# A three-number VectorE instruction in a new shape, and the first batch's softmax weights four slots later, in a fused attention and MLP kernel

## The chip, the cores and the metric

The kernel runs on one core of a Trainium2 chip. The metric is the time of one execution on the device in microseconds (us), as the median of several executions. Ratios are the mean time of one kernel's runs over that of the kernel before in the same rounds on the same chip, so they are not quite the ratio of the medians quoted beside them.

The engines are called PE (TensorE matmul), PEld (its weight load), DVE (VectorE), ACT (ScalarE) and POOL (GpSimd).

## The reference

```python
scores = scale * q @ k.T                          # 8 batches, 8 heads, 576 x 576, depth 64
thresh = max(scores, axis=-1) - tau
scores = where(scores >= thresh, scores, -1e9)
attn = exp(scores - max(scores)); attn /= sum(attn) + 1e-9
x = (attn @ v), heads side by side                # 4608 x 512
h = x @ w_in;  out = (h - tanh(h)) @ w_out        # hidden width 2048
```

## The kernel before

The work is a list of 288 score tiles (128 query rows by 576 keys), nine for each pair of heads. One slot of the schedule handles several tiles at different stages: in slot s the scores of tile s+8 are made, the threshold shift `nb` of tile s+7, the kinked scores `z` of tile s+5, and the transposes and the exponential of tile s; the product with V follows two slots later. In the first batch these last three are done four slots earlier. From the second batch on, the MLP of the batch before is mixed in, so PE has much more to do. GpSimd splits K and Q into two fp16 halves, swaps halves of K^T (`kS`), casts V, and casts the MLP's weights.

The parts that the change touches:

```python
mx = const.tile([P, 3], F32, name=f"mx{i}")       # row maxima: tile A in column 0, tile B in column 1
...
def shift(i):                                     # once for two tiles A and B, or for one tile M
    kd = kind(i % TPP)
    if kd == "A":
        return
    n = 3 if kd == "B" else 1
    mx = mxs.pop(i)
    nb = st_pool.tile([P, 3], F32, name="nb", tag="nb")
    nc.vector.tensor_scalar(
        out=nb[:, 0:n], in0=mx[:, 0:n], scalar1=-1.0, scalar2=tau,
        op0=ALU.mult, op1=ALU.add,
    )
    nbs[i] = nb[:, n // 2 : n // 2 + 1]
    if kd == "B":
        nbs[i - 1] = nb[:, 0:1]
...
for i in range(NTILE + 3):
    at = i - 4 if i < HPAIR * TPP else i          # slot of the weights; the first batch is 36 tiles
    atts.setdefault(at + LAG, []).append(i)
    if i < NTILE:
        wts.setdefault(at, []).append(i)
...
```

## Time and profile before

| | before |
|---|---|
| median of the first three runs | 549.77 us (549.69 to 550.95) |
| the run that was profiled | 543.29 us, span of the core 541.5 us |
| PE, DVE, ACT, POOL busy | 94, 82, 81, 54% |
| `nb` instructions | 160, 45.6 us in all, 136 to 1240 ns each |

### The profile page before, as it was taken

How to read it: one execution, taken by the hardware profiler on the slowest of the kernel's cores; microseconds unless marked ns; L12 is line 12 of the kernel's file. 1: busy time of each engine (PE TensorE's matmuls, PEld its weight loads, DVE VectorE, ACT ScalarE, POOL GpSimd, SP SyncE). 2: the span in 40 equal slices, each digit the busy share in tenths (PEclk: the TensorE clock that was granted, in tenths of full speed). 3: DMA queues.
4: the chain of work that ended last, by engine and by line, in shares of the span. 5: the costliest groups of instructions: out<-in, count | busy, mean ns of one | idle time of the engine just before them, and what ended most of it. 6: DMA issues, size and time to landing. Idle time of an engine off the chain costs nothing.

```text
span 541.5 us, 12959 instructions
## 1 busy us (share of the span) xinstructions
PE 506.7 (94%) x4704; PEld 288.0 (53%) x4771; DVE 445.9 (82%) x1203; ACT 438.3 (81%) x628; POOL 291.1 (54%) x390
## 2 busy tenths in 40 slices
PE   5999898989999999999999999999999999999997
PEld 3666565555555555555555555555555455444444
DVE  4999988989988999889888998899888887554440
ACT  4999888999898989899888989898989989533330
POOL 7999996767555666666545654566665620000000
PEclk9999999999999999999999999999999999999999
DMA  7554657999898998889999899698969975301113
GB/s 207 174 183 146 205 179 141 184 186 170 196 186 151 185 188 189 161 179 184 185 185 183 182 187 197 154 181 185 188 165 182 197 148 105 101 20 40 39 41 78
DMA packets 204768, 85.76 MB, mean 158 GB/s; under 512 B 172320, under 2 KB 197152, under 8 KB 204704
## 3 DMA queue, kind: packets, MB, share of 16 engines
q1 hardware_dynamic: 204112, 84.51, 72.6%
q8 instruction: 37, 0.61, 0.5%
q10 hardware_dynamic: 592, 0.43, 0.3%
q14 instruction: 27, 0.22, 0.1%
HBM read 36.70 MB, written 9.44 MB: 85 GB/s over the span
## 4 chain that ended last, share of the span: by engine, by line
PE 62%; DVE 24%; issue 5%; ACT 5%; DMA 3%; SPq 0%; DVEq 0%; ACTq 0%; POOL 0%
PE psY L510 18%; PE psH L484 16%; PE psS L319 13%; DVE sc L329 12%; PE psO L429 4%; DVE g L503 4%; PE psS L309 3%; PE ps_k L233 2%; PE psHt L484 2%; ACT pT L392 2%; ACT z L363 2%; DVE yo L520 2%; DMA qT<-qhl 2%; DVE nb L343 2%; DVE kT L256 1%
## 5 line engine op out<-in xcount | busy, mean ns | idle before, releaser
L329 DVE TENSOR_SCALAR_CACHE_REDUCE sc<-psS 128x576 f32<-128x576 f32 x288 | 215.7, 751 | 17.7 <-PE psS L319 10.4
L363 ACT ACTIVATE z<-sc,nb 128x576 bf16<-128x576 f32 x256 | 194.0, 771 | 22.9 <-DVE nb L343 22.4
L262 POOL COPY kS<-kT 64x1152 f16<-64x1152 f16 x62 | 70.9, 1143 | 132.6 <-DVE nb L343 130.9
L510 PE MATMUL psY<-w_out_sb,g 128*128 128x512 bf16 (+1 forms) x551 | 137.4, 373 | 4.1 <-DVE yo L520 1.6
L400 ACT ACTIVATE pT<-zT 128x1152 f16<-128x1152 bf16 (+1 forms) x130 | 139.1, 1070 | 0.0
L484 PE MATMUL psH<-xT,w_in_sb 128*128 128x512 bf16 x455 | 119.2, 379 | 7.2 <-DVE g L503 3.9
L319 PE MATMUL psS<-kT,qT 128*128 128x512 f16 (+1 forms) x512 | 104.9, 286 | 8.5 <-DVE sc L329 6.5
L497 ACT ACTIVATE th<-psH 128x512 f32<-128x512 f32 x128 | 75.5, 590 | 38.3 <-PE psH L484 37.7
L319 PEld LDWEIGHTS <-qT 128*128 128x128 f16 x1024 | 72.8, 97 | 58.1 <-issue 11.6
L503 DVE SCALAR_TENSOR_TENSOR g<-th,psH 128x512 bf16<-128x512 f32 x128 | 87.3, 682 | 19.0 <-ACT th L497 18.8
L319 PE MATMUL psS<-kS,qT 128*128 128x512 f16 x496 | 101.4, 286 | 0.0
L510 PEld LDWEIGHTS <-g 128*128 128x128 bf16 x592 | 50.7, 98 | 58.2 <-issue 5.7
L484 PEld LDWEIGHTS <-w_in_sb 128*128 128x128 bf16 x576 | 49.2, 98 | 59.7 <-issue 6.0
L429 PEld LDWEIGHTS <-pT 128*128 128x128 f16 x1280 | 55.7, 98 | 25.3 <-issue 1.7
L429 PE MATMUL psO<-vb,pT 128*128 128x65 bf16 x1280 | 61.2, 193 | 0.3
L343 DVE TENSOR_SCALAR nb<-mx 128x3 f32<-128x3 f32 (+1 forms) x160 | 45.6, 285 | 2.3
L186 POOL TENSOR_TENSOR khl<-kraw,khl 128x576 f16<-128x576 f32 x31 | 39.7, 1281 | 2.6
L186 POOL TENSOR_TENSOR qhl<-qraw,qhl 128x576 f16<-128x576 f32 x31 | 39.7, 1280 | 2.6
L392 ACT ACTIVATE pT<-psZ 128x640 f16<-128x640 bf16 (+1 forms) x54 | 35.4, 658 | 5.2 <-PE psZ L383 4.8
L256 DVE COPY kT<-ps_k 128x1152 f16<-128x1152 f16 x31 | 23.4, 756 | 13.3 <-PE ps_k L233 13.3
L520 DVE COPY yo<-psY 128x512 f32<-128x512 f32 (+1 forms) x33 | 22.5, 681 | 12.2 <-PE psY L510 7.6
L444 DVE TENSOR_TENSOR osb<-psO,rc 128x256 bf16<-128x256 f32 x64 | 27.2, 425 | 2.2
(78 smaller groups left out, 504.6 us busy)
## 6 DMA issues: line engine op xcount, KB each, us to landing
vraw<-in_v_dram SPq DMA_DIRECT2D x32, 256.0 KB, 3.5
out_dram<-yo SPq DMA_DIRECT2D x32, 256.0 KB, 2.8
kraw<-in_k_dram SPq DMA_DIRECT2D x31, 256.0 KB, 3.1
qraw<-in_q_dram SPq DMA_DIRECT2D x31, 256.0 KB, 3.9
wt<-in_moe_w_in_dram SPq DMA_DIRECT2D x8, 512.0 KB, 4.8
wt<-in_moe_w_out_dram SPq DMA_DIRECT2D x8, 512.0 KB, 3.9
zT<-z SPq DMA_TRANSPOSE x104, 3.5
kraw<-in_k_dram SPq DMA_DIRECT2D x32, 32.0 KB, 3.1
```

What stands on the lines that cost most here:

```text
L186: nc.gpsimd.tensor_tensor(out=hl[:, :, 1, :], in0=x, in1=hl[:, :, 0, :], op=ALU.subtract)
L262: nc.gpsimd.tensor_copy(out=o, in_=i)
L319: nc.tensor.matmul(out=ps[:, dst], lhsT=lhs, rhs=kk[:, src], start=(n == 0), stop=(n == 1),)
L329: nc.vector.tensor_scalar(out=sc, in0=ps[:, lo : lo + S], scalar1=SC, scalar2=None, op0=ALU.mult, op1=ALU.max, accum_out=mx[:, c : c + 1],)
L343: nc.vector.tensor_scalar(out=nb[:, 0:n], in0=mx[:, 0:n], scalar1=-1.0, scalar2=tau, op0=ALU.mult, op1=ALU.add,)
L363: nc.scalar.activation(out=z, in_=sc, func=ACT.Prelu, bias=nb, scale=1.0, alpha=STEEP)
L400: nc.scalar.activation(out=pt[:, 0 : n * P], in_=zts.pop(i)[:, 0:n, :], func=ACT.Exp)
L429: nc.tensor.matmul(out=po[:, (j - 1 - 5 * hh) + ab, :], lhsT=pt[:, blk * P : (blk + 1) * P], rhs=vb[:, hh, c, :], start=(n == 0), stop=(n ...
L484: nc.tensor.matmul(out=ps, lhsT=w_in_sb[:, c, n * P : (n + 1) * P], rhs=xs[m][:, c, :] if m < B else xR[:, c, :, :], start=(c == 0), stop= ...
L497: nc.scalar.activation(out=th, in_=ps, func=ACT.Tanh)
L503: nc.vector.scalar_tensor_tensor(out=gs[m][:, n, :], in0=th, scalar=-1.0, in1=ps, op0=ALU.mult, op1=ALU.add,)
L510: nc.tensor.matmul(out=ps, lhsT=gs[m][:, n, ms * P : (ms + 1) * P], rhs=w_out_sb[:, n, cols], start=(n == 0), stop=(n == DF_C - 1),)
```

## The change

It has two parts. The first writes the shift of a pair of tiles as rows: three numbers in each of two input rows, two in each of three output rows, of which only the first two outputs are used. The maxima get eight columns so that the input rows exist. The second moves the weights of the first batch to the slots that the other batches use.

```diff
-        mx = const.tile([P, 3], F32, name=f"mx{i}")
+        mx = const.tile([P, 8], F32, name=f"mx{i}")
...
-        n = 3 if kd == "B" else 1
         mx = mxs.pop(i)
-        nb = st_pool.tile([P, 3], F32, name="nb", tag="nb")
+        nb = st_pool.tile([P, 9], F32, name="nb", tag="nb")
+        o, m = nb[:, 0:1], mx[:, 0:1]
+        if kd == "B":
+            o = nb.rearrange("p (a b) -> p a b", b=3)[:, :, 0:2]
+            m = mx.rearrange("p (a b) -> p a b", b=4)[:, :, 0:3]
         nc.vector.tensor_scalar(
-            out=nb[:, 0:n], in0=mx[:, 0:n], scalar1=-1.0, scalar2=tau,
-            op0=ALU.mult, op1=ALU.add,
-        )
-        nbs[i] = nb[:, n // 2 : n // 2 + 1]
+            out=o, in0=m, scalar1=-1.0, scalar2=tau, op0=ALU.mult, op1=ALU.add
+        )
         if kd == "B":
-            nbs[i - 1] = nb[:, 0:1]
+            nbs[i - 1], nbs[i] = nb[:, 0:1], nb[:, 1:2]
+        else:
+            nbs[i] = nb[:, 0:1]
...
-        at = i - 4 if i < HPAIR * TPP else i
+        at = i - 0 if i < HPAIR * TPP else i
```

## The prediction

> **What bounds the kernel now.** I read the page first, then the list of groups, the rows of one line, the timeline around single instructions, the chain, and the waits by stretch. The page says that no engine has much room:
>
> ```profile
> PE 506.7 (94%) x4704; PEld 288.0 (53%) x4771; DVE 445.9 (82%) x1203; ACT 438.3 (81%) x628; POOL 291.1 (54%) x390
> ...
> L343 DVE TENSOR_SCALAR nb<-mx 128x3 f32<-128x3 f32 (+1 forms) x160 | 45.6, 285 | 2.3
> ```
>
> The reader is to see two things. PE is nearly always busy, so whatever DVE saves can only be taken out of PE's few holes. And an instruction that makes three numbers per partition takes 285 ns on average, far too much for its size. Busy time by stretch:
>
> ```profile
> core 0: us, PE busy (x) PEld busy (x) DVE busy (x) ACT busy (x) POOL busy (x), PEclk, DMA share, GB/s
> ...
> 16.00:60.00 44.00, 40.11 (x565) 28.45 (x564) 42.47 (x122) 42.58 (x69) 41.69 (x52) 1.00 0.57 178
> 60.00:125.00 65.00, 57.87 (x634) 36.24 (x641) 58.11 (x164) 58.71 (x89) 49.98 (x63) 1.00 0.76 166
> 125.00:460.00 335.00, 323.68 (x3020) 180.79 (x3070) 302.65 (x831) 300.05 (x413) 186.87 (x238) 1.00 0.89 177
> 460.00:542.00 82.00, 75.36 (x406) 36.25 (x409) 33.99 (x57) 28.48 (x46) 0.00 (x0) 0.99 0.18 53
> ```
>
> There are three regimes. From 16 to 60 us (the first batch, attention alone) ACT and DVE are both near 97% and PE has 3.9 us of holes. From 125 to 460 PE has 11.3 us of holes in 335. After 460 there are no `nb` instructions and PE runs alone.
>
> Now the rows of line 343, where the duration spreads over a factor of nine, and one instance in the timeline:
>
> ```profile
> L343 DVE TENSOR_SCALAR nb<-mx x160: 136/169/1240, 10.4 to 459.4; 128x3 f32<-128x3 f32 x128, 128x1 f32<-128x1 f32 x32
> ```
>
> ```profile
> 270.78 1.28 POOL L186 TENSOR_TENSOR qhl<-qraw,qhl 128x576 f16<-128x576 f32 x1
> ...
> 271.01 1.07 DVE L343 TENSOR_SCALAR nb<-mx 128x3 f32<-128x3 f32 x1
> ...
> 271.99 0.74 DVE L329 TENSOR_SCALAR_CACHE_REDUCE sc<-psS 128x576 f32<-128x576 f32 x1
> ...
> 272.67 0.68 DVE L520 COPY yo<-psY 128x512 f32<-128x512 f32 x1
> ...
> 273.27 0.67 DVE L503 SCALAR_TENSOR_TENSOR g<-th,psH 128x512 bf16<-128x512 f32 x1
> ...
> 273.99 0.38 PE L484 MATMUL psH<-xT,w_in_sb 128*128 128x512 bf16 x1 [0.70 <-DVE g L503]
> ```
>
> The GpSimd subtraction ends at 272.06 and the `nb` that began inside it ends at 272.08. Then three DVE instructions stand back to back and PE idles 0.70 us for the last of them. I went through all 160 in the timeline. The 32 of one element take 0.14 to 0.15 us, every one. Of the 128 of three elements, 82 take 0.15 to 0.20 us and 46 take 0.25 us or more; nearly all of those 46 end within 0.04 us after a GpSimd instruction ends. With 0.165 us for an undisturbed one, the three-element rows (128 x 0.320 = 41.0 us) hold 41.0 - 128 x 0.165 = 19.8 us of waiting for GpSimd: some 5 us of it before 70 us, the rest later.
>
> [...] the 3-to-3 form is held up, 46 times in 128, until a GpSimd instruction ends; the 1-to-1 form never is, 0 times in 32.
>
> **Part one, the new shape.** The instruction order shows the same 160 `nb`, now 128x3x2 out, with an input of two rows of three. [...] It computes six numbers in place of three (two are used), which I put at the 0.14 us of the one-element form or slightly more: 0.15 us. DVE work removed: 128 x (0.320 - 0.15) = 21.8 us, so L343 should fall from 45.6 to about 24 us and DVE from 446 to about 424.
>
> What does this buy? Not 21.8 us: I take only what lies on the chain that ended last. Its pieces on line 343 longer than an undisturbed one are:
>
> ```profile
> 23.39 0.60 DVE nb L343
> ...
> 34.68 0.68 DVE nb L343
> ...
> 108.79 0.67 DVE nb L343
> ...
> 153.38 0.43 DVE nb L343
> ...
> 209.28 1.24 DVE nb L343
> ...
> 271.01 0.44 DVE nb L343
> ```
>
> and after these 206.99 (0.32), 329.84 (0.44) and 389.07 (0.43). Where the piece is a cut of a longer instruction (153, 271, 330, 389) the whole piece is waiting; from the others I take 0.165 off. Sum after 70 us: 0.50 + 0.43 + 0.16 + 1.08 + 0.44 + 0.44 + 0.43 = **3.5 us**. Before 70 us: 0.44 + 0.52 = **0.96 us**. The other waits lie where DVE afterwards waits for PE anyway. Since the chain without these pieces is still a chain of the program, 4.4 us is about the most that this part can give while the order and the other durations stay.
>
> **Part two, the first batch's weights four slots later.** The transposes of tile i (line 383), the exponential (392) and the product with V (429) move from slot i-4 to slot i for the first 36 tiles. No instruction is added; only the order on PE and ACT changes. Now the transposes come one slot after the ACT instruction that makes `z`, and PE[...] stands waiting. Waits from 16 to 60 us:
>
> ```profile
> PEld L383 <- ACT z L363: 5.0, 14, 0.7
> ...
> PE psS L319 <- DVE sc L329: 2.1, 6, 0.5
> PE psZ L383 <- ACT z L363: 1.4, 4, 0.4
> ```
>
> After the change `z` is five slots old and these waits should be gone. The bound is then ACT: on the chain an ACT `z` takes 0.67 us to the next instruction and a `pT` 0.50 to 0.60. From 16 to 60 us it runs 35 `z` and 34 `pT`: 35 x 0.67 + 34 x 0.54 = 41.8 of 44 us. So only 2.2 us are to be had there. A little more lies in slots -4 to -1, which the timeline puts at 13.1 to 18.5 us: 5.4 us with `pT` in them, by my estimate 4.6 us if they hold only scores; slots 32 to 35, now with `z` alone, get their `pT` back and stay at about 5.2 us. I take **2.5 us** for the first batch with both parts together, the 0.96 us included. Sum: 3.5 + 2.5 = 6.0 us, and 0.4 us for shorter undisturbed `nb` on the chain: 549.8 - 6.4 = **543.4 us**.
>
> **Rivals.**
> First, DVE relief is worth far more, as DVE is at 97% in the first batch and 90% later: if most of PE's holes from 16 to 460 us (3.9 + 7.1 + 11.3 = 22.3 us) close, the time falls to 530 or lower. For it: DVE frees 22 us. Against it: most of those holes name other causes (`psS` waiting for `sc` where no `nb` was held, `psH` for `xT`, `pT`).
> Second, ACT takes over at once and nothing comes of it: about 549. For it: ACT already has 97% in the first batch and 90% later. Against it: the chain has PE at 62%, DVE at 24% and ACT at 5%.
> Third, the deferral costs: ACT runs short of work in slots -4 to -1 and has the same `pT` to do later, so the first batch grows by 1 to 2 us and the sum is near 547.
> Fourth, a transfer: DMA share is 0.89 in the long stretch and `qT` by DMA lies on the chain twice, 5.55 and 3.98 us. But PE's waits for it are only a few tenths of a us, so I expect at most 1 us either way.
>
> **Range and chances.** The parts bound the gain at about 3.9 us (first batch) plus 4 (later) plus 1.5 (DMA and small things), so 540; if the deferral costs and the chain gives half, 547.5. Two per cent faster is below 538.8, past what I can add up: 10%. Slower by over 2% has no mechanism: 2%. Within: 88%.
>
> **What would show it.** L343 with a maximum below 0.25 us, a mean near 0.15, and a sum near 24; no `nb` that ends with a GpSimd instruction. DVE near 424 us. The waits of L383 for `z` before 60 us gone. The scores of tile 45 (`sc` at 64.75 us now) some 2.5 us earlier; the end of the last `nb` (459.4 now) some 6 us earlier; the stretch after it unchanged at about 82 us. The prediction is wrong if long `nb` remain[...], if the first batch does not shorten (part two costs what part one gives), or if PE's holes from 125 to 460 us fall by more than 5 us.

What the first profile shows is this: 44 of the three-element `nb` began inside a GpSimd instruction that had more than 0.25 us still to run, and all 44 were held, for 0.28 to 1.24 us; five of one element began so, and none took more than 0.154 us. That the new shape would behave like the one-element form was not shown before the result; here it is the author's assumption.

## More of the kernel before

The lines of the profile itself stand in the prediction. One more, from the page, is needed later; it gives the share of each engine on the chain of work that ended last:

```profile
PE 62%; DVE 24%; issue 5%; ACT 5%; DMA 3%; SPq 0%; DVEq 0%; ACTq 0%; POOL 0%
```

The reader is to see DVE with a quarter of the chain and POOL with nothing.

## The result, and the profile after

The changed kernel takes 539.98 us (539.28 to 541.02, six runs) against 549.82 us (549.69 to 550.95, six runs) before: 9.8 us less, ratio 0.9818 (0.9806 to 0.9831). Its profiled run took 539.28 us with a span of 537.5 us. So the **timed** runs differ by 9.8 us, but the two **profiles** by 541.5 - 537.5 = 4.0 us only.

From the page after, the line of the engines and then that of the chain's engines:

```profile
PE 509.6 (95%) x4771; PEld 288.0 (54%) x4771; DVE 428.3 (80%) x1203; ACT 436.2 (81%) x628; POOL 290.3 (54%) x390
...
PE 67%; DVE 15%; POOL 7%; ACT 5%; issue 4%; DMA 3%; SPq 0%; DVEq 0%; POOLq 0%; ACTq 0%
```

DVE lost 17.6 us of busy time and 9 points of the chain; POOL, which was not on the chain, now has 7%. The rows of the new `nb` (minimum, median and maximum in ns):

```profile
L347 DVE TENSOR_SCALAR nb<-mx x160: 142/153/161, 10.8 to 455.4; 128x6 f32<-128x6 f32 x128, 128x1 f32<-128x1 f32 x32
```

The spread is gone: no `nb` takes longer than 161 ns. The timeline after, at the place that the prediction showed of before:

```profile
268.70 1.28 POOL L187 TENSOR_TENSOR qhl<-qraw,qhl 128x576 f16<-128x576 f32 x1
...
268.98 0.16 DVE L347 TENSOR_SCALAR nb<-mx 128x6 f32<-128x6 f32 x1
...
270.24 0.69 DVE L524 COPY yo<-psY 128x512 f32<-128x512 f32 x1
...
271.58 1.02 PE L488 MATMUL psH<-xT,w_in_sb 128*128 128x512 bf16 x4 [0.32 <-DVE g L507]
```

Again `nb` begins inside the GpSimd subtraction, but now it ends after 0.16 us, with the subtraction still running for 0.8 us. It is not the only one: 61 of the 128 new ones began inside a GpSimd instruction with more than 0.25 us to run, and none of the 61 took more than 160 ns. PE's hole is 0.32 us where it was 0.70.

Where the 4.0 us came from is read by laying the starts of the 288 `sc` instructions of the two timelines side by side. The scores of tile 36 start 0.8 us earlier than before, those of tile 45 at 64.74 us where they started at 64.75, those of tile 282 start 4.0 us earlier, and the last `nb` at 455.4 us in place of 459.4. So the first batch gained 0.8 us and lost it again, and the whole gain between the profiles was made after 65 us. (Such a comparison needs care: in the profiles tile 8 starts up to 0.7 us before or 1.8 us after that of the first profile, unchanged kernels included. For these two the difference is 0.2 us. Counted from tile 8 the shape alone, in e2_shape and e12_shape_again below, also gains 0.4 us by tile 36 and has none of it left at tile 45.) Busy time in the first batch and in the long stretch after, then waits in the first batch:

```profile
16.00:60.00 44.00, 39.75 (x563) 28.86 (x562) 38.84 (x121) 40.87 (x68) 41.70 (x52) 1.00 0.58 183
125.00:460.00 335.00, 329.84 (x3096) 182.39 (x3095) 293.62 (x835) 303.04 (x418) 185.66 (x238) 1.00 0.90 179
```

```profile
PEld L234 <- POOL qhl L187: 2.3, 3, 1.4
...
PE ps_q L234 <- POOL qhl L187: 1.8, 3, 1.2
...
PEld L234 <- POOL khl L187: 1.2, 2, 1.0
```

From 16 to 60 us DVE fell from 42.5 to 38.8 us and ACT from 42.6 to 40.9, but POOL stands at 41.7 of 44 us as before, and the waits for `z` (5.0 and 1.4 us) have given way to waits of PE for GpSimd's halves of Q and K. From 125 to 460 us the rows put PE's holes at 335 - 329.8 = 5.2 us, after 11.3 before. Not all of this is a gain: the first trace lacks 67 of the 4771 matmul records. In e5_look_a, the same kernel with all of them, PE is busy for 326.6 of these 335 us, so the holes were 8.4 us and the fall is about 3 us.

### The profile page after: what moved, and what is told of

Same layout as the page of the kernel before. It is cut to its first block, busy times and chain, and to the rows that moved or that the text cites. A ratio compares the mean times of both kernels' runs of the same rounds, so it can differ in the third digit from the quotient of the medians. Undisturbed runs are those within 1.5% of the kernel's fastest.

```text
span 537.5 us, 13027 instructions
## 1 busy us (share of the span) xinstructions
PE 509.6 (95%) x4771; PEld 288.0 (54%) x4771; DVE 428.3 (80%) x1203; ACT 436.2 (81%) x628; POOL 290.3 (54%) x390
## 4 chain that ended last, share of the span: by engine, by line
PE 67%; DVE 15%; POOL 7%; ACT 5%; issue 4%; DMA 3%; SPq 0%; DVEq 0%; POOLq 0%; ACTq 0%
PE psY L514 20%; PE psH L488 18%; PE psS L320 14%; DVE sc L330 6%; PE psO L433 5%; DVE g L507 3%; PE psS L310 3%; PE ps_k L234 2%; PE psHt L488 2%; ACT z L367 2%; DVE yo L524 2%; POOL kS L263 2%; DVE kT L257 2%; POOL w_in_sb L618 1%; ACT pT L396 1%
## 5 line engine op out<-in xcount | busy, mean ns | idle before, releaser
L514 PE MATMUL psY<-w_out_sb,g 128*128 128x512 bf16 (+1 forms) x592 | 146.0, 374 | 1.6 <-DVE yo L524 1.6
L488 PE MATMUL psH<-xT,w_in_sb 128*128 128x512 bf16 x480 | 124.0, 379 | 2.3 <-DVE g L507 2.3
L234 PE MATMUL ps_k<-ident_f,khl 128*128 128x128 f16 x288 | 22.0, 221 | 7.0 <-DVE khl L200 5.8
```

The source lines that it names most:

```text
L488: nc.tensor.matmul(out=ps, lhsT=w_in_sb[:, c, n * P : (n + 1) * P], rhs=xs[m][:, c, :] if m < B else xR[:, c, :, :], start=(c == 0), stop= ...
L514: nc.tensor.matmul(out=ps, lhsT=gs[m][:, n, ms * P : (ms + 1) * P], rhs=w_out_sb[:, n, cols], start=(n == 0), stop=(n == DF_C - 1),)
```

## The experiments

Eighteen runs were made. Each is of the kernel before or the changed one, as it stands or with the edit shown, and every one gave correct results. A "look" is one profiled execution without timed runs.

### Taking the change apart

The first four ran on one chip. `e1_same` is the kernel before, unchanged. `e2_shape` is the changed kernel with the slots put back, `e3_slots` the kernel before with the new slots alone:

```diff
-        at = i - 0 if i < HPAIR * TPP else i     # e2_shape, from the changed kernel
+        at = i - 4 if i < HPAIR * TPP else i
```

`e4_six_even` is the changed kernel with the output written as two rows of three, like the input:

```diff
-            o = nb.rearrange("p (a b) -> p a b", b=3)[:, :, 0:2]
+            o = nb[:, 0:8].rearrange("p (a b) -> p a b", b=4)[:, :, 0:3]
```

> The kernel before, unchanged, to see whether its profiled run (543.3 us) is a luckier run than its timed ones (549.8). Theory A (the length of the waits for GpSimd depends on how the two engines' instructions happen to line up, and the profiled run lined up well): timed runs near 549.8 again, and if a profile or any run of this kernel falls in the ordinary state, the rows of line 343 hold clearly more than 45.6 us and more pieces of them lie on the chain. Rival (the profile shortens or the first trace was cut): every profile of it is 541 to 542 us long with 45 to 46 us on line 343, while the timed runs stay at 549.8.

> The new shape alone, first batch's weights still four slots early. Theory A: the shape makes nearly all of the gain, so 540 to 542 us and a ratio of 0.982 to 0.987, all nb under 0.2 us. Rival B (the later slots make the 6 us that the two traces do not show): 545 to 547 us.

> The later slots alone, with the old shape of three in and three out. Theory A: 548 to 551 us, no gain, with long nb as before. Rival B: 543 to 545 us.

> The changed kernel, but its six numbers are written as two rows of three from two rows of three[...]. Theory A[...]: long nb of up to 1.2 us are back and the time is that of the later slots alone, 548 to 551 us. Rival (the strided layout or six elements in place of three matter): no long nb, near 540 us.

| run | median | lowest to highest |
|---|---|---|
| kernel before, same rounds | 544.17 | 543.23 to 550.63 (11 runs) |
| e1_same | 548.48 | 544.93 to 550.52 |
| e2_shape | 538.62 | 537.83 to 539.00 |
| e3_slots | 548.05 | 545.17 to 552.81 |
| e4_six_even | 546.88 | 546.25 to 551.37 |

The rows of `nb` in e4_six_even, whose partner in time is e3_slots (the same slots), and then in e2_shape:

```profile
L347 DVE TENSOR_SCALAR nb<-mx x160: 141/170/1230, 10.9 to 462.9; 128x6 f32<-128x6 f32 x128, 128x1 f32<-128x1 f32 x32
```

```profile
L347 DVE TENSOR_SCALAR nb<-mx x160: 141/152/163, 10.9 to 455.2; 128x6 f32<-128x6 f32 x128, 128x1 f32<-128x1 f32 x32
```

Six elements from two rows of three in both, and 1230 ns against 163: it is the output's rows, two of three (four elements apart) against three of two (three apart), that decide, not the size. Why they do is in no view of the profile. The shape makes the whole gain and the slots alone make none, so rival B falls. And a new fact stands in the last column: the three kernels in which `nb` can be held vary by 5 to 8 us from run to run on one chip, and the one in which it cannot varies by 1.2 us. Neither theory for e1_same fits fully: its profiled run took 544.93 us and had an ordinary 45.4 us on line 343, so it did not show a long run from inside.

### Looking for a profile of a long run

Three looks at the kernel before, without edit, and beside them a second form that should not be held: `e8_ones` writes the shift of a pair as two instructions of one element each.

```diff
...
-            out=o, in0=m, scalar1=-1.0, scalar2=tau, op0=ALU.mult, op1=ALU.add
...
+        for c in range(2 if kd == "B" else 1):
+            nc.vector.tensor_scalar(out=nb[:, c : c + 1], in0=mx[:, c : c + 1], ...)
```

> The kernel before again, one look, to catch a profile of one of its runs near 550 us. Theory A2 (each batch of the long stretch has a close race[...], at the nb that starts within some 10 ns of the GpSimd copy of V; when GpSimd wins, an nb some 2 us later is held for 1.23 us): if the look is near 550 us, its trace shows nb of 1.2 us in four to seven of the seven batches, against one in the traces of 541.5 and 543.1 us; if it is near 544, one or two. Rival (the slow runs come from the loads or the clock): a trace near 550 us has the same nb as the others.

> As e5_look_a: near 550 us four to seven nb of 1.2 us, near 544 us one or two. The rival expects the same nb at either time.

> As e5_look_a: near 550 us four to seven nb of 1.2 us, near 544 us one or two. The rival expects the same nb at either time.

> The shift of a pair of tiles as two instructions of one element each, which never waited for GpSimd; the first batch's weights four slots early, so e2_shape is its partner. Theory A: as fast as the new shape, 538 to 541 us and within 1.5 us from run to run, although DVE does 128 instructions[...] more. Rival (what counts is that DVE has less to do): about 3 us above e2_shape.

On this chip the kernel before took 549.32 to 551.26 us in nine timed runs, but the three looks took 543.74, 545.47 and 545.58 us: the long runs escaped the profile again, and the looks are no test of A2. e8_ones took 538.78 us (537.89 to 539.11), ratio 0.9786, level with e2_shape although DVE ran 128 more instructions and was busy for 297.4 us from 125 to 460 us, where it has 293.5 in e2_shape. Its longest `nb` takes 156 ns. So having less for DVE to do is not what counts; not being held is.

The looks weaken A2 all the same. In the first profile the `nb` at 206.99 us and a GpSimd copy of V at 207.00 start together, GpSimd wins (the `nb` takes 0.32 us and ends 0.02 us after the copy), and the next `nb` is held for 1.24 us; one batch later the same `nb` wins (it takes 0.17 us, and the copy 0.32 in place of 0.29) and the next takes 0.17 us. In e5_look_a GpSimd won one batch earlier than in the first profile, yet from tile 108 to tile 234 the two start within 0.06 us of one another, but for a few tiles just behind the race that the first profile lost: the `nb` after the held one, 1.06 us in a normal batch, took 0.21 and made the loss good. After the second batch e6_look_b lost this race in no batch and e7_look_c in two, and their spans are 543.7 and 543.8 us.

### Setting the race by hand

`e9_gpsimd_first` delays DVE ahead of that `nb` in every second pair, `e10_vector_first` delays GpSimd inside the copies of V instead:

```diff
+    late = const.tile([P, 1], F32, name="late")                   # both
...
+        if i % TPP == 6 and i // TPP % 2 == 0 and i // TPP > 4:    # e9, in shift
+            nc.vector.memset(late, 0.0)
+        if p % 2 == 1 and p > 4:                                   # e10, in split_v
+            nc.gpsimd.memset(late, 0.0)
```

`e11_after` and `e12_shape_again` are the changed kernel and e2_shape, beside each other. (The expectation of e11 says tile 28; it means slot 28, where tile 36 is scored. That of e9 says fourteen `nb`; the edit reaches thirteen. Its 60 ns are those of a one-element DVE memset in the first profile, 59 ns; GpSimd's of one element take 96 to 103 ns there.)

> The kernel before with a one-element memset (some 60 ns) put ahead of fourteen nb (every second pair of heads, the tile whose nb begins within 10 ns of a GpSimd copy of V in the traces), so that GpSimd should win that race each time. Theory A2 (this race makes the slow runs): all runs at 549 to 552 us, and the profile shows an nb of 1.2 us after each. Rival A3 (the race is made good afterwards: in the traces an nb of 1.24 us is followed by one of 0.2 where 1.06 stood, and the later tiles are not shifted): profile still near 544, timed runs 543 to 551 as before.

> The kernel before with a small GpSimd memset (some 100 ns) inside the copies of V of the same pairs, so that DVE should win that race each time. Theory A2: all runs near 543 us within 1.5 us. Rival A3: timed runs spread from 543 to 551 us as before, whatever the profile shows.

> The changed kernel on the same chip as its partner e12_shape, which differs only in the slots. If the later slots cost what the first batch's traces say (0.7 us gained by tile 28, lost again by tile 45): equal within 0.5 us; from the runs on different chips (539.98 against 538.62): 1.0 to 1.5 us slower than e12_shape.

> The new shape with the weights four slots early, beside e11_after on one chip: 538 to 539 us, 1.0 to 1.5 us faster than e11_after if the later slots cost time, equal if they do not. All runs within 1.5 us in either case.

| run | median | lowest to highest | ratio |
|---|---|---|---|
| kernel before, same rounds | 544.67 | 543.73 to 545.50 (11 runs) | |
| e9_gpsimd_first | 544.42 | 543.72 to 545.97 | 1.0000 |
| e10_vector_first | 542.50 | 541.99 to 542.61 | 0.9958 |
| e11_after | 540.42 | 539.54 to 541.26 | 0.9924 |
| e12_shape_again | 539.08 | 538.64 to 539.53 | 0.9898 |

On this chip the kernel before never reached 546 us, and the changed kernel gains only 544.67 - 540.42 = 4.3 us. e9 cost nothing, but it is no clean test: its profile shows GpSimd winning that race only once after the first two batches, as without the edit. Theory A2, that this one race makes the long runs, was set aside for the reason just told, that a lost race is made good. e10 is the surprise of the set: a GpSimd memset of some 0.1 us saved 2.2 us and took most of the spread away. Its trace shows where part of that comes from. In four batches the `nb` second after that race (at 242.5, 300.9, 359.2 and 417.6 us) takes 0.17 us, where the first profile has 0.67 or 0.68, and tile 252, which starts 0.9 us earlier than in the first profile, had lagged 0.5 us at tile 153. The delay did not win a race so much as let other `nb` go free: the phase of the two engines as a whole seemed to matter. The later slots cost 540.42 - 539.08 = 1.3 us against their partner on the same chip (the two profiled runs, with spans of 538.0 and 537.7 us, show only 0.3 of it).

### Moving the phase, with `nb` that can be held and without

From the seventh pair on, the turn of K (its transposition on PE, after which GpSimd can swap the halves of K^T) comes one slot later (turn4) or earlier (turn6). This moves the phase, that is, where GpSimd's instructions fall between those of DVE. The order of GpSimd's instructions stays the same. The edit is made to the kernel before, where `nb` took up to 1.24 us, and to e2_shape, where none took more than 163 ns. The labels call the first locked and the second free; "lock" there and in the expectations is only a name for what was measured, that an `nb` is held until a GpSimd instruction ends:

```diff
             d -= p == 1 and d in (3, 5)
+            if d == 5 and p > 5:
+                d = 4                            # or 6
```

> The kernel before with the turn of K one slot later from the seventh pair on; the order on GpSimd stays, but its work starts at another phase of DVE's, so other nb collide. Theory A4 (with the waits[...] the time depends on that phase; the runs near 550 us are a bad phase): the time moves by 2 us or more from the kernel before's, and more than between the two lock-free partners; the sum of the nb rows differs by 5 us or more from 45.6. Rival A5 (the 550 us come from something else, the phase is worth little): within 1.5 us of the kernel before.

> The same with the turn of K one slot earlier. Theory A4: another time again, 2 us or more away from the kernel before or from e13_locked_turn4, between 540 and 552 us. Rival A5: within 1.5 us of the kernel before.

> The new shape (weights four slots early) with the turn of K one slot later: no nb waits. Theory A4: 537.5 to 540 us, within 1.5 us from run to run, so that a change of phase alone costs nothing without the lock. Rival A5: it moves as e13_locked_turn4 does.

> The new shape with the turn of K one slot earlier. Theory A4: 537.5 to 540 us as e15_free_turn4. Rival A5: it moves as e14_locked_turn6 does.

| turn of K | `nb` can be held (locked) | never held (free) |
|---|---|---|
| one slot later | 550.71 (550.10 to 551.50) | 540.33 (539.99 to 540.54) |
| one slot earlier | 543.22 (542.86 to 544.58) | 538.38 (537.93 to 539.41) |
| as it was, same rounds | 550.65 (549.63 to 551.24) | not run here |

With `nb` that can be held, two slots of phase are worth 7.5 us; without, 2.0 us. Read across, the shape saves 10.4 us at one phase and 4.8 us at the other, on one chip. At last there is a profile of 549.7 us of a kernel with held `nb`. From e13_locked_turn4, the three-element `nb` (busy us and mean ns), and then busy time in the long stretch:

```profile
L343 DVE TENSOR_SCALAR nb<-mx 128x3 f32<-128x3 f32 x128 | 58.0, 453 | 2.3
```

```profile
125.00:460.00 335.00, 324.16 (x3016) 177.73 (x3016) 311.89 (x819) 293.46 (x405) 189.18 (x242) 1.00 0.88 176
```

The three-element rows hold 58.0 us against 41.0 in the first profile of the kernel before: 17 us more waiting, spread over 68 held instructions in place of 46. DVE is at 93% of the long stretch where it was at 90%, and the batches there fall behind those of the first profile by 0.9 us each (slots 112 to 220: from 3.7 to 6.4 us late in three batches). e14_locked_turn6 has 47.8 us in those rows, more than the first profile, and still takes 543.2 us: so it seems to count which `nb` are held, and not only how long.

### Relieving GpSimd in the first batch

`e17_casts_late` is e2_shape with six to eight of the casts of the MLP's weights moved to the second batch, `e18_casts_late_slots` is the same with the later slots:

```diff
-    w_when = [4 * i + 3 for i in range(17)]
+    w_when = [3, 11, 19, 27] + [38 + 3 * i for i in range(13)]
...
```

and the first halves of w_in are loaded ahead of the second ones.

> The new shape with the weights four slots early (e12_shape_again, 538.6 to 539.1 us), and six to eight of GpSimd's casts of the MLP's weights (1.04 us each) moved from the first batch to the second, where GpSimd has room. Theory (GpSimd, at 41.7 of 44 us, and ACT both sit at the limit in the first batch): GpSimd's share from 16 to 60 us falls by 5 us or more and the time by 0 to 2 us, as ACT at 43 of 44 us then holds it: 537 to 539 us. Rival (GpSimd's share there costs nothing): no change.

> The same casts moved, with the weights at their usual slots, partner of e17_casts_late and of the changed kernel (540.0 to 540.4 us). Theory (the later slots took PE's waits for z away and GpSimd's qhl and khl took their place, so the slots gain only if GpSimd is relieved): PE's waits for qhl and khl before 60 us are gone and the time is 537 to 538.5 us, 1.5 us or more below the changed kernel. Rival (the later slots cost time for a reason of their own, such as ACT being short of work in the first four slots): still 1 us or more above e17_casts_late.

They took 542.64 us (541.85 to 543.14) and 542.04 us (541.14 to 542.87): both slower than e12_shape_again and the changed kernel (other chips, with a clock of 0.998 to 1.0 where it was 0.994 to 0.997 here; the kernel before had 0.998 to 1.0 on this chip too), so neither expectation of a time held, and GpSimd's 41.7 us from 16 to 60 us fell only to 38.9 and 40.3. But the first batch answers the question. In e18_casts_late_slots the waits of PE for GpSimd's `qhl` and `khl` are gone from the list for 16 to 60 us, and the scores of slots 40 to 64 start 1.8 us earlier than in the changed kernel; without the later slots (e17 against e12_shape_again) the same casts are worth 0.4 us there. So it was GpSimd that the later slots ran into. (The casts take their loads with them, so the transfers were relieved too: the DMA share from 16 to 60 us is 0.43, and 0.58 in the changed kernel; but the waits that went had named GpSimd.) The medians point the same way: with GpSimd relieved the later slots are 0.6 us quicker than their partner on the same chip, though the ranges overlap, where without it they were 1.3 us slower. The loss comes later, in the stretch from 60 to 125 us of e18:

```profile
PE psS L320 <- DMA qT<-qhl: 3.0, 1, 3.0
```

The first transpose of Q by DMA comes 3.0 us too late for PE where the weights' loads now fall (DMA share 0.84 from 60 to 125 us, 0.76 in the changed kernel); by slot 76 the kernel is 1.9 us behind. The same wait stands in e17_casts_late. That the loads delay the transpose was not tested.

The quickest kernel is the shape without the slots: e2_shape, e12_shape_again, and, with the turn of K moved, e16_free_turn6 at 538.38 us. Its ratios to the kernel before are 0.9856, 0.9898 and 0.9774; the spread of these is that of the kernel before, not theirs.

## Why the prediction was wrong

**The held `nb` and their cure: right.** The rows should fall to about 24 us with a mean near 0.15 us and a maximum below 0.25. They measured 19.9 + 4.6 = 24.5 us, 155 ns for the six-element form, and at most 161 ns. e4_six_even shows that the output's rows are the cause (up to 1230 ns with two rows of three), and in e8_ones another form that was never held (at most 156 ns) does as well. DVE as a whole fell to 428.3 us, not to 424; the rest was not followed up.

**The gain after the first batch: right in the profiles.** The chain's pieces gave 3.5 us, and 0.4 us for shorter `nb`: 3.9 us. The profiles show 4.0 us between tile 45 and the end; that it is so close is partly luck, as the same stretch gained 3.5 us in e11_after, 3.6 in e12_shape_again and 4.8 in e2_shape. The sign "PE's holes from 125 to 460 us fall by more than 5 us" came by the printed rows alone (11.3 to 5.2 us), through the missing records told above. The place shown from the timeline gave 0.70 - 0.32 = 0.38 us for a piece of 0.44.

**The first batch: wrong.** The step "I take **2.5 us** for the first batch" failed: the profiles show 0.0 us at tile 45, with the shape's 0.96 us not to be seen there either, and against e12_shape_again the later slots cost 1.3 us. The waits for `z` went as predicted, but I named ACT as the bound there and overlooked, in the row that I had printed myself, POOL with 41.69 of 44 us. Once DVE and ACT were ahead, GpSimd set the pace, which e18 supports. The third rival had the sign right, but for another reason. Two readings there were loose, without effect on the sum: the product with V moves from slot i-2 to i+2, and after 460 us PE does not run alone (DVE is busy for 34.0 of the 82 us, ACT for 28.5).

**The sum: wrong, and this decided it.** The step that made the forecast time wrong is "549.8 - 6.4 = **543.4 us**". It takes from a time of 549.8 us what a trace of a 543.3 us run says, and so treats 6.5 us of the kernel before as if they would stay. They did not: the changed kernel's timed runs agree with its profile. The remark that 4.4 us is about the most that the first part can give holds for the run that was traced, not for the runs that were timed. On the chip where the kernel before ran at its profile's level, the gain was 4.3 us, with 6.4 predicted; where it ran at 549.8, it was 9.8.

**What the 6.5 us are.** Shown: of all the kernels here only those whose `nb` can be held ever took 545 us or more; the same form, which can be held, takes 550.7 or 543.2 us by a shift of phase alone; with forms that never were, the runs of a kernel agree within 1.8 us on each chip. (On four of the six sets the kernel before did so too; a spread of 5 to 8 us was seen on the other two, and only where `nb` can be held.) Argued, not shown: that the long runs of the kernel before are such a phase. No profile of the unchanged kernel fell on one; the spans of all five were 541.5 to 543.8 us. What sends it to one level or the other from run to run and from chip to chip (549 to 551 us in all timed runs of three sets, 543 to 546 in one, both in two) stays open. So does a rival: that taking a profile itself favours the lower level. All seven profiles of kernels whose runs reached 549 us and more in some runs and not in others (the unchanged kernel, e3_slots, e4_six_even) have spans of 541.5 to 545.0 us; e13 shows only that a profiled run can be long.

## What to carry to other kernels

When a trace of one run is to explain a time, check first that this run took that time; a saving read from a trace cannot be taken from a longer run without asking where the rest is. If a tiny VectorE instruction spreads in duration by a factor of nine beside a busy GpSimd, look whether its long instances end with a GpSimd instruction. Here they did: 45 of the 46 of the first trace end within 0.04 us after one. A shape that was never held cured the cost, and on the chips where there was one, the run-to-run spread. Four forms were tried. Three to three and two rows of three to two rows of three were held, for 1.29 and 1.23 us at most; one to one and two rows of three to three rows of two never were, at 145 and 155 ns on average. What a shape does elsewhere has to be measured there. Before naming the next bound, read every engine's column of the stretch, also that of an engine with no share of the chain.
